# Experts of a top-1 mixture computed once each on 224 slots, with rows scattered to per-expert regions in DRAM

## The chip, the core and the metric

The kernel runs on one core of one Trainium2 chip. The metric is device time in microseconds (us) for one execution. Five engines work side by side, each with its own instruction queue: TensorE (PE; PEld is its weight load), VectorE (DVE), ScalarE (ACT), GpSimd (POOL) and SyncE (SP, which here only issues DMAs). Sixteen DMA engines move the data that the queues of SP, ACT and POOL ask for.

## The reference

Gated linear attention over 4 batches x 8 heads x 768 steps with head size 48, then a mixture of 16 experts in 4 groups of 4. Every one of 3072 tokens (rows of 384 numbers) goes to one expert, all in float32.

```python
for t in range(S):
    state = alpha[:, :, t, :, None] * state + np.einsum('bhd,bhe->bhde', k[:, :, t], v[:, :, t])
    y[:, :, t] = np.einsum('bhd,bhde->bhe', q[:, :, t], state)
x = y.transpose(0, 2, 1, 3).reshape(B * S, H * D)        # 3072 x 384

g_idx = np.argmax(x @ w_group, axis=1)                   # softmax weight g_w
e_idx = np.argmax(xg @ w_expert[g], axis=1)              # softmax weight e_w
h = np.maximum(xg[mask_e] @ w1[g, e], 0.0)               # 384 -> 1024
out[tok_idx] = (g_w * e_w)[:, None] * (h @ w2[g, e])     # 1024 -> 384
```

## The kernel before

**Attention.** Sixteen passes (a batch and a pair of heads each) run in a row. `load` brings q, k and alpha of a pass on SP's queue into one of two buffers. `decayed` forms the decay products: DVE scans alpha (line 150) and takes reciprocals, GpSimd makes `qp`, `ka` and half of `ks`, DVE makes `kp` and the rest. `scores`, `states` and `outputs` are matmuls on TensorE in chunks of 128 steps; `scores` needs `ka`, and `states` needs `ks`. Each matmul on float32 leaves two records in the trace. Results go to `x`, a tile of 128 rows x 6 chunks per batch, with two buffers.

**Gates.** After four passes `gates` computes a batch's routing: logits, the best group and expert, the weight (column 384 of `x`), `picked` (one-hot of 16) and `rank`, a token's place among those of its expert. The whole `x` of the batch is written to `x_dram` by one DMA from GpSimd (line 295).

**Slots.** When all tokens are ranked, DVE sorts them into 39 tiles of 128 slots: tile e below 16 has the first 128 tokens of expert e, and 23 more tiles take what is left of any expert, enough for every way in which the tokens can fall. Products of one-hots give the token of each slot (lines 400 to 425).

**Experts.** For every tile, GpSimd gathers its rows with an indirect DMA (`fetch_rows`, three tiles ahead), TensorE turns them (`turned`), and multiplies by `w1` (24 matmuls of 128 columns, line 466) and, after ReLU on ACT, by `w2` (8 matmuls of 384 columns, line 474). DVE scales the result into `yo`, and an indirect DMA scatters it to the output (line 479); slots without a token point beyond the output and write nothing. `load_weights` on SP's queue brings the weights of a tile, 1536 KB for each layer, into one of three buffers; the first three sets are requested during the attention passes. All 39 tiles are computed, whether they hold tokens or not.

**Order.** A scheduler in the library lays out each engine's queue ahead of time; it may move an instruction forward past others of its engine. Within a queue the order is then fixed. It also adds the waits: an instruction that writes what an earlier one wrote or reads waits for it, a DMA's write until it has landed.

Of the kernel before, what the change touches and what calls it, by code (L numbers as in the profile page):

```python
# [19 lines left out]
P = 128  # L20
# [4 lines left out]
def gla_then_hierarchical_moe(  # L25
# [9 lines left out]
    """Gated linear attention in chunks of 128 steps, then a top-1 of 4x4 expert MoE.  # L35

    The decay products restart every 64 steps, so that their reciprocals stay in range; a
    chunk's two segments are joined by the first one's whole decay.

    Tokens are sorted by expert into tiles of 128 slots: tile e < NE has the first 128 tokens of  # L40
    expert e, and the NX tiles after those have what is left of any expert, whose weights are
    fetched by its index. NX covers every way in which the tokens can fall.
    """
# [16 lines left out]
    NX = NT - 1  # L60
    NS = NE + NX
    XW = DM + 1
# [11 lines left out]

    x_dram = dp.tile([N, XW], F32, name="x_dram")
    x_rows = x_dram.rearrange("(b c p) w -> b p c w", b=B, p=P)

# [23 lines left out]
    lane_f = iota("lane_f", [P, P], [[1, P]])  # L101
    tile_f = iota("tile_f", [P, NT], [[1, NT]])
    full_f = iota("full_f", [P, NX], [[P, NX]], base=P)
# [6 lines left out]
    rank = cp.tile([P, NT], F32, name="rank")  # L110
    eid = cp.tile([P, NT], F32, name="eid")
# [15 lines left out]
    with ExitStack() as gla:  # L127
# [50 lines left out]
        def states(j, v, ks, tot):  # L178
            """The state before chunks 1, 2, ..., as blocks of the two heads."""
# [64 lines left out]
        def gates(b, x):  # L244
# [18 lines left out]
            def first_best(z, name):  # L263
                """The first best of four as one-hot, and the sum of exp(z - best)."""
# [30 lines left out]
            nc.gpsimd.dma_start(out=x_rows[b], in_=x)  # L295

            cs = slice(b * NC, (b + 1) * NC)
            ix = sp.tile([P, NC], F32, name="ix")
            nc.vector.tensor_scalar(out=ix, in0=gix[:, :, 0], scalar1=-4.0, scalar2=20.0,
                                    op0=ALU.mult, op1=ALU.add)  # L300
            nc.vector.tensor_tensor(out=eid[:, cs], in0=ix, in1=eix[:, :, 0], op=ALU.subtract)
# [19 lines left out]
            nc.vector.tensor_reduce(out=rank[:, cs], in_=rk, axis=AX.X, op=ALU.add)  # L321
# [10 lines left out]
        for j in range(PAIRS):  # L332
            b, hp = divmod(j, HP)
            if j + 1 < PAIRS:
                load(j + 1)
            if hp == 0:
                xs[b] = xp.tile([P, NC, XW], F32, name="x")
                if b + 1 < B:
                    load_v(b + 1)
            if j in (2, 4, 6):  # L340
                load_weights(j // 2 - 1, j // 2 - 1)
            qp, kp, qs, ks, ka, tot = decayed(j)
            sm = scores(0, qp, kp, ka)
            st = states(j, vs[b], ks, tot)
            for c0 in range(0, NC, 2):
                nxt = scores(c0 + 2, qp, kp, ka) if c0 + 2 < NC else None
                outputs(j, c0, sm, qs, st, vs[b], xs[b])
                sm = nxt
            if hp == HP - 1:
                gates(b, xs[b])  # L350

# [1 line left out]
    mp = ctx.enter_context(tc.tile_pool(name="moe", bufs=2))  # L353
    rp = ctx.enter_context(tc.tile_pool(name="route", bufs=1))

    cnt = seen[:, NT, :]
# [8 lines left out]
    base = rp.tile([P, NE], F32, name="base")  # L365
    nc.vector.tensor_tensor(out=base, in0=ends, in1=more, op=ALU.subtract)

# [5 lines left out]
    whose_i = rp.tile([P, NX], I32, name="whose_i")  # L373
    nc.vector.tensor_scalar(out=whose_i, in0=whose, scalar1=float(NE - 1), scalar2=None,
                            op0=ALU.min)

    turn3 = rp.tile([P, NT, NX], F32, name="turn3")
    nc.vector.tensor_tensor(out=turn3, in0=rank[:, :, None].to_broadcast([P, NT, NX]),
                            in1=full_f[:, None, :].to_broadcast([P, NT, NX]), op=ALU.is_ge)
    turn = rp.tile([P, NT], F32, name="turn")  # L380
    nc.vector.tensor_reduce(out=turn, in_=turn3, axis=AX.X, op=ALU.add)
    lo = rp.tile([P, NT], F32, name="lo")
    nc.vector.scalar_tensor_tensor(out=lo, in0=turn, scalar=-float(P), in1=rank, op0=ALU.mult,
                                   op1=ALU.add)
    own3 = rp.tile([P, NT, NE], F32, name="own3")
    nc.vector.tensor_tensor(out=own3, in0=picked, in1=base[:, None, :].to_broadcast([P, NT, NE]),
                            op=ALU.mult)
    hi = rp.tile([P, NT], F32, name="hi")
    nc.vector.tensor_reduce(out=hi, in_=own3, axis=AX.X, op=ALU.add)
    nc.vector.scalar_tensor_tensor(out=hi, in0=hi, scalar=float(NE - 1), in1=turn, op0=ALU.add,  # L390
                                   op1=ALU.add)
    late = rp.tile([P, NT], F32, name="late")
    nc.vector.tensor_scalar(out=late, in0=turn, scalar1=1.0, scalar2=None, op0=ALU.min)
    nc.vector.tensor_tensor(out=hi, in0=hi, in1=eid, op=ALU.subtract)
    nc.vector.tensor_tensor(out=hi, in0=hi, in1=late, op=ALU.mult)
    nc.vector.tensor_tensor(out=hi, in0=hi, in1=eid, op=ALU.add)

    # The token of each slot: a product of one-hots, whose numbers are whole and below 256.
    los = rp.tile([P, NT, P], BF16, name="los")
    nc.vector.tensor_tensor(out=los, in0=lo[:, :, None].to_broadcast([P, NT, P]),  # L400
                            in1=lane_f[:, None, :].to_broadcast([P, NT, P]), op=ALU.is_equal)
    his = rp.tile([P, NT, 3, NS], BF16, name="his")
    nc.vector.tensor_tensor(out=his[:, :, 0, :], in0=hi[:, :, None].to_broadcast([P, NT, NS]),
                            in1=lane_f[:, None, 0:NS].to_broadcast([P, NT, NS]), op=ALU.is_equal)
    nc.vector.tensor_scalar(out=his[:, :, 1, :], in0=his[:, :, 0, :], scalar1=part_f,
                            scalar2=None, op0=ALU.mult)
    nc.vector.tensor_tensor(out=his[:, :, 2, :], in0=his[:, :, 0, :],
                            in1=tile_f[:, :, None].to_broadcast([P, NT, NS]), op=ALU.mult)
    zs = bank()
    for t in range(NT):  # L410
        nc.tensor.matmul(zs[:, 0:3 * NS], lhsT=los[:, t, :],
                         rhs=his[:, t].rearrange("p k s -> p (k s)"), start=(t == 0),
                         stop=(t == NT - 1))
    slot = rp.tile([P, 3, NS], F32, name="slot")
    nc.vector.tensor_copy(out=slot, in_=zs[:, 0:3 * NS].rearrange("p (k s) -> p k s", k=3))
    tok = rp.tile([P, NS], F32, name="tok")
    nc.vector.scalar_tensor_tensor(out=tok, in0=slot[:, 2, :], scalar=float(P), in1=slot[:, 1, :],
                                   op0=ALU.mult, op1=ALU.add)
    src_i = rp.tile([P, NS], I32, name="src_i")
    nc.vector.tensor_copy(out=src_i, in_=tok)  # L420
    none = rp.tile([P, NS], F32, name="none")
    nc.vector.tensor_scalar(out=none, in0=slot[:, 0, :], scalar1=-float(N), scalar2=float(N),
                            op0=ALU.mult, op1=ALU.add)
    dst_i = rp.tile([P, NS], I32, name="dst_i")
    nc.vector.tensor_tensor(out=dst_i, in0=tok, in1=none, op=ALU.add)  # L425

# [1 line left out]
    def fetch_rows(i):  # L428
        xg = mp.tile([P, XW], F32, name="xg", bufs=4)
        nc.gpsimd.indirect_dma_start(  # L430
            out=xg, out_offset=None, in_=x_dram,
            in_offset=bass.IndirectOffsetOnAxis(ap=src_i[:, i:i + 1], axis=0),
            bounds_check=N - 1, oob_is_err=False)
        return xg

    def fetch_weights(i):
        if i < NE:
            return load_weights(i, i)
        e = nc.values_load(whose_i[0:1, i - NE:i - NE + 1], engines=[ENG.SP], min_val=0,
                           max_val=NE - 1,  # L440
                           skip_runtime_bounds_check_because="an index of one of NE")
        load_weights(i, e)

    def turned(xg):
        z = bank()
        for dc in range(DC):
            nc.tensor.transpose(z[:, dc * P:(dc + 1) * P], xg[:, dc * P:(dc + 1) * P], ident)  # L447
        xt = mp.tile([P, DC, P], F32, name="xgt")
        nc.vector.tensor_copy(out=xt.rearrange("p c t -> p (c t)"), in_=z[:, 0:DM])  # L449
        return xt  # L450

    AHEAD = 3
    rows = {i: fetch_rows(i) for i in range(AHEAD)}
    xt = turned(rows[0])
    for i in range(NS):
        if i + AHEAD < NS:
            rows[i + AHEAD] = fetch_rows(i + AHEAD)
        w1, w2 = weights.pop(i)
        xg = rows.pop(i)
# [62 lines left out]
```

## Time and profile before

| | |
|---|---|
| median of three runs | 971.7 us (971.56 to 972.98) |
| profiled execution: span from first to last instruction | 967.5 us |
| TensorE matmul busy | 862.4 us, 89% |
| VectorE busy | 314.5 us, 33% |
| GpSimd busy | 148.9 us, 15% |
| bytes moved by DMA | 159.4 MB |

The profile is of one execution, and its page gives the span alone as that execution's own time; the runs are timed around the whole program. Busy times are per engine and overlap. A stretch of the span is read from a table of windows, a single place from the timeline, and the time that a DMA takes from its issue to its landing from the list of DMAs.

### The profile page before, as it was taken

How to read it: one execution, taken by the hardware profiler on the slowest of the kernel's cores; microseconds unless marked ns; L12 is line 12 of the kernel's file. 1: busy time of each engine (PE TensorE's matmuls, PEld its weight loads, DVE VectorE, ACT ScalarE, POOL GpSimd, SP SyncE). 2: the span in 40 equal slices, each digit the busy share in tenths (PEclk: the TensorE clock that was granted, in tenths of full speed). 3: DMA queues.
4: the chain of work that ended last, by engine and by line, in shares of the span. 5: the costliest groups of instructions: out<-in, count | busy, mean ns of one | idle time of the engine just before them, and what ended most of it. 6: DMA issues, size and time to landing. Idle time of an engine off the chain costs nothing. (4 is left out here: it accounts for less than half of the span.)

```text
span 967.5 us, 10908 instructions
## 1 busy us (share of the span) xinstructions
PE 862.4 (89%) x4413; PEld 695.5 (72%) x4413; DVE 314.5 (33%) x785; ACT 91.8 (9%) x211; POOL 148.9 (15%) x151
## 2 busy tenths in 40 slices
PE   0499987999879998699991999999999999999996
PEld 0377775777757777477781788877887788778884
DVE  0856656345563454934316010101011010101010
ACT  0000010000100001000010001100111001100110
POOL 2211111101111010110001122111211121111200
PEclk9999999999999999555555999999999999999998
DMA  9732233202331022300001689988998888999940
GB/s 331 202 103 37 37 85 87 38 0 38 86 85 38 1 37 37 87 1 0 1 1 63 212 317 332 329 324 326 325 334 316 325 307 326 314 314 316 317 164 1
DMA packets 20130, 159.44 MB, mean 165 GB/s; under 512 B 3976, under 2 KB 4022, under 8 KB 8048
## 3 DMA queue, kind: packets, MB, share of 16 engines
q1 hardware_dynamic: 13280, 136.85, 43.8%
q0 software_dynamic: 6080, 17.15, 5.0%
q10 hardware_dynamic: 720, 4.75, 1.3%
q8 instruction: 35, 0.57, 0.2%
q14 instruction: 15, 0.12, 0.1%
HBM read 149.28 MB, written 12.40 MB: 167 GB/s over the span
## 5 line engine op out<-in xcount | busy, mean ns | idle before, releaser
L466 PEld LDWEIGHTS bank<-xgt,w 128*128 128x128 f32 x1872 | 216.8, 193 | 11.1 <-DVE xgt L449 1.1
L466 PE MATMUL bank<-xgt,w 128*128 128x128 f32 x1872 | 217.2, 276 | 0.7 <-DVE xgt L449 0.7
L474 PE MATMUL bank<-w,hT 128*128 128x384 f32 x624 | 207.7, 486 | 0.0
L214 PE MATMUL bank<-qp,kp 48*128 48x128 f32 x384 | 147.1, 498 | 35.1 <-DVE tot L175 35.1
L474 PEld LDWEIGHTS bank<-w,hT 128*128 128x128 f32 x624 | 115.5, 190 | 72.3
L214 PEld LDWEIGHTS bank<-qp,kp 48*128 48x128 f32 x384 | 92.5, 308 | 59.7 <-issue 38.6
L237 PE MATMUL bank<-v,sm 128*128 128x48 f32 x384 | 98.0, 401 | 0.0
L237 PEld LDWEIGHTS bank<-v,sm 128*128 128x128 f32 x384 | 93.0, 329 | 4.8 <-issue 1.6
L479 POOL DMA_INDIRECT out_dram<-yo,dst_i x39 | 39.6, 1016 | 340.7 <-DVE yo L477 340.7
L216 PE MATMUL bank<-qp,ka 48*64 48x64 f32 x384 | 87.5, 337 | 0.1
L449 DVE COPY xgt<-bank 128x384 f32<-128x384 f32 x39 | 21.7, 558 | 200.3 <-PE bank L447 200.3
L220 DVE TENSOR_TENSOR sm<-bank,causal 128x256 f32<-128x256 f32 x96 | 39.8, 421 | 142.4 <-PE bank L216 141.1
L468 ACT ACTIVATE hT<-bank 128x512 f32<-128x512 f32 x78 | 46.6, 597 | 397.3 <-PE bank L466 397.3
L477 DVE TENSOR_SCALAR yo<-bank,xg 128x384 f32<-128x384 f32 x39 | 24.1, 618 | 184.9 <-PE bank L474 184.9
L216 PEld LDWEIGHTS bank<-qp,ka 48*64 48x64 f32 x384 | 52.6, 200 | 39.8 <-issue 38.1
L152 DVE RECIPROCAL inv<-cum 112x768 f32<-112x768 f32 x16 | 79.2, 4952 | 0.5
L155 POOL TENSOR_TENSOR qp<-qka,cum 112x768 f32<-112x768 f32 x16 | 28.9, 1805 | 216.1 <-issue 81.3
L232 PE MATMUL bank<-state,qs 112*128 112x96 f32 x160 | 53.9, 456 | 0.0
L150 DVE TENSOR_TENSOR_SCAN cum<-qka,zeros 112x64 f32<-112x64 f32 x192 | 41.8, 272 | 25.4 <-DMA qka<-in_qka_dram 25.4
L194 PE MATMUL bank<-v,kn 128*112 128x96 f32 x160 | 39.9, 415 | 9.0 <-ACT kn L190 9.0
L194 PEld LDWEIGHTS bank<-v,kn 128*112 128x112 f32 x160 | 32.3, 298 | 16.4 <-ACT kn L190 14.6
L430 POOL DMA_INDIRECT xg<-x_dram,src_i x39 | 39.6, 1014 | 28.0 <-DVE dst_i L425 16.4
(108 smaller groups left out, 432.5 us busy)
## 6 DMA issues: line engine op xcount, KB each, us to landing
w<-in_w_dram SPq DMA_DIRECT2D x78, 1536.0 KB, 9.1
qka<-in_qka_dram SPq DMA_DIRECT2D x32, 432.0 KB, 7.0
x_dram<-x POOLq DMA_DIRECT2D x4, 1155.0 KB, 6.4
v<-in_v_dram ACTq DMA_DIRECT2D x4, 1152.0 KB, 9.1
xg<-x_dram,src_i POOLq DMA_INDIRECT x39, 7.3
out_dram<-yo,dst_i POOLq DMA_INDIRECT x39, 7.9
wr<-in_wr_dram ACTq DMA_DIRECT2D x1, 30.0 KB, 7.1
```

Source lines behind the costliest of these rows:

```text
L150: nc.vector.tensor_tensor_scan(out=cum[:, sl], data0=a[:, sl], data1=zeros[0:R], initial=1.0, op0=ALU.mult, op1=ALU.add)
L152: nc.vector.reciprocal(out=inv, in_=cum)
L194: nc.tensor.matmul(z[0:R, c * D2:(c + 1) * D2], lhsT=kn[:, i, :], rhs=v[:, c, hp * D2:(hp + 1) * D2], start=True, stop=True)
L214: nc.tensor.matmul(z[:, o:o + P], lhsT=kp[r, c:c + P], rhs=qp[r, c:c + P], start=True, stop=True)
L216: nc.tensor.matmul(z[0:SEG, o + SEG:o + P], lhsT=ka[r, c // 2:c // 2 + SEG], rhs=qp[r, c + SEG:c + P], start=True, stop=True)
L220: nc.vector.tensor_tensor(out=s, in0=z[:, 0:2 * P].rearrange("p (c i) -> p c i", c=2), in1=causal[:, None, :].to_broadcast([P, 2, P]), op= ...
L232: nc.tensor.matmul(z[:, i * D2:(i + 1) * D2], lhsT=qs[:, c * P:(c + 1) * P], rhs=st[0:R, c - 1, :], start=True, stop=False, skip_group_che ...
L237: nc.tensor.matmul(z[:, i * D2 + t * D:i * D2 + (t + 1) * D], lhsT=sm[t][:, i, :], rhs=v[:, c, h * D:(h + 1) * D], start=(c == 0 and t == ...
L430: nc.gpsimd.indirect_dma_start(out=xg, out_offset=None, in_=x_dram, in_offset=bass.IndirectOffsetOnAxis(ap=src_i[:, i:i + 1], axis=0), bou ...
L466: nc.tensor.matmul(z[:, k * P:(k + 1) * P], lhsT=w1[:, dc, f * P:(f + 1) * P], rhs=xt[:, dc, :], start=(dc == 0), stop=(dc == DC - 1))
L468: nc.scalar.activation(out=hT[:, f0:f0 + 4, :].rearrange("p f t -> p (f t)"), in_=z, func=AF.Relu)
L474: nc.tensor.matmul(zy[:, 0:DM], lhsT=hT[:, f, :], rhs=w2[:, f, :], start=(f == 0), stop=(f == FC - 1))
```

## The change

- `x` gets a second extra column with the token's number. The write of `x` to `x_dram` goes. `gates` now computes `place` = expert x 3072 + rank for each token, and six indirect DMAs per batch scatter the rows of `x` to `slots_d`, a region of 3072 rows per expert in DRAM.
- The first 224 rows of each of these regions are set to zero beforehand by one DMA from `blank`, written in the pass j = 1.
- The one-hot routing goes. Each expert is computed once, on the first 224 rows of its region, in parts of 128 and 96 rows, which plain DMAs on ACT's queue load. `hidden` runs w1 on 224 columns at once, with four evictions of 448 columns; `result` runs w2 for each part. `drop` sends slots beyond an expert's count past the end of the output.
- Tokens of an expert beyond 224 are left to a loop with a run-time count, a tile of 128 rows per pass. Its bookkeeping stands on DVE.

```diff
-    NX = NT - 1
-    NS = NE + NX
-    XW = DM + 1
+    CAP = 224
+    NX = -(-(N - CAP) // P)
+    XW = DM + 2
-    x_dram = dp.tile([N, XW], F32, name="x_dram")
+    slots_d = dp.tile([NE * N, XW], F32, name="slots_d")
+    blank = cp.tile([P, 2 * XW], F32, name="blank")
+    nc.vector.memset(blank, 0.0)
...
-            nc.gpsimd.dma_start(out=x_rows[b], in_=x)
+            nc.vector.tensor_copy(out=x[:, :, DM + 1], in_=token_f[:, cs])
...
+            nc.vector.scalar_tensor_tensor(out=place, in0=ix, scalar=float(N), in1=rank,
+                                           op0=ALU.mult, op1=ALU.add)
+            for c in range(NC):
+                nc.gpsimd.indirect_dma_start(
+                    out=slots_d, out_offset=bass.IndirectOffsetOnAxis(ap=place[:, c:c + 1], axis=0),
+                    in_=x[:, c, :], in_offset=None, bounds_check=NE * N - 1, oob_is_err=False)
...
+            if j == 1:
+                nc.sync.dma_start(
+                    out=slots_d.rearrange("(e n) w -> e n w", e=NE)[:, 0:CAP, :].rearrange(
+                        "e (p t) w -> p e (t w)", t=2),
+                    in_=blank[0:CAP // 2, None, :].to_broadcast([CAP // 2, NE, 2 * XW]))
...
+    def hidden(w1, xt, n):
+        hT = mp.tile([P, FC, CAP], F32, name="hT")
+        for f0 in range(0, FC, 2):
+            z = bank()
+            for k in range(2):
+                f = f0 + k
+                for dc in range(DC):
+                    nc.tensor.matmul(z[:, k * n:(k + 1) * n], lhsT=w1[:, dc, f * P:(f + 1) * P],
+                                     rhs=xt[:, dc, 0:n], start=(dc == 0), stop=(dc == DC - 1))
+            nc.scalar.activation(out=hT[:, f0:f0 + 2, 0:n],
+                                 in_=z[:, 0:2 * n].rearrange("p (f t) -> p f t", f=2), func=AF.Relu)
...
+    halves = [(0, P), (P, CAP - P)]
+    def fetch_rows(e):
+        xg = mp.tile([P, 2, XW], F32, name="xg", bufs=4)
+        for t, (c0, n) in enumerate(halves):
+            nc.scalar.dma_start(out=xg[0:n, t, :], in_=slots_d[e * N + c0:e * N + c0 + n, :])
...
+    for e in range(NE):
+        if e + AHEAD < NE:
+            rows[e + AHEAD] = fetch_rows(e + AHEAD)
...
+        hT = hidden(w1, xt, CAP)
+        if e + 1 < NE:
+            xt = columns(rows[e + 1])
+        for t, (c0, n) in enumerate(halves):
+            result(w2, hT, c0, n, xg[0:n, t, DM:DM + 1], dst[0:n, t:t + 1])
+        if e + 3 < NE:
+            load_weights(e + 3, e + 3)
...
+    n_left = nc.values_load(n_more[0:1, 0:1], min_val=0, max_val=NX,
+                            skip_runtime_bounds_check_because="a count of at most NX")
+    with tc.For_i(0, n_left) as i:
...
```

The queue of SP at the program's start, before. `w` is a weight tile of either layer, `qka` the tile of q, k and alpha:

```order
L120 DMA w_383<-in_w_dram 128x3072
L122 DMA w_384<-in_w_dram 128x3072
L120 DMA w_753<-in_w_dram 128x3072
L141 DMA qka_114<-in_qka_dram 48x2304 [waits Pool_49]
L141 DMA qka_114<-in_qka_dram 48x2304
```

The same place in SP's queue after the change:

```order
L120 DMA w_386<-in_w_dram 128x3072
L348 DMA slots_d<-blank 112x16x772 [waits DVE_49]
L141 DMA qka_116<-in_qka_dram 48x2304 [waits Pool_49]
L141 DMA qka_116<-in_qka_dram 48x2304
```

The zeroing of the slots stands second, although it is written in pass j = 1, and two of the weight transfers stand behind the first `qka` loads.

GpSimd's queue in the passes behind the third batch, before; `Pool`, `DVE`, `PE` and `Activation` in the waits are engines, DMASW and DMAHW semaphores of DMAs:

```order
L169 TENSOR_TENSOR ka<-kp,cum 112x384 [waits DVE_49]
L295 DMA x_dram<-x 128x6x385 [waits DVE_49,Activation_49]
L171 TENSOR_TENSOR ks<-ka,cum 112x6x64 [waits Pool_49]
L155 TENSOR_TENSOR qp<-qka_114,cum 112x768 [waits DMAHW0_49,DMAHW7_49,DVE_49,PE_49]
L169 TENSOR_TENSOR ka<-kp,cum 112x384 [waits DVE_49]
L171 TENSOR_TENSOR ks<-ka,cum 112x6x64 [waits Pool_49]
```

The same passes after the change, up to the six scatters of the last batch (the first two of them are shown):

```order
L171 TENSOR_TENSOR ks<-ka,cum 112x6x64 [waits Pool_49]
L326 DMA slots_d<-x,place 49152x386 [waits DMASW3_49,DVE_49,Activation_49]
L326 DMA slots_d<-x,place 49152x386 [waits DMASW4_49]
L155 TENSOR_TENSOR qp<-qka_116,cum 112x768 [waits DMAHW0_49,DMAHW1_49,DVE_49,PE_49]
L326 DMA slots_d<-x,place 49152x386 [waits DMASW5_49,Activation_49]
L326 DMA slots_d<-x,place 49152x386 [waits DMASW6_49]
L326 DMA slots_d<-x,place 49152x386 [waits DMASW7_49,Activation_49]
L169 TENSOR_TENSOR ka<-kp,cum 112x384 [waits DVE_49]
L171 TENSOR_TENSOR ks<-ka,cum 112x6x64 [waits Pool_49]
L326 DMA slots_d<-x,place 49152x386 [waits DMASW0_49]
```

One DMA has become six, with `qp`, `ka` and `ks` of the next pass between them, and each scatter waits for the semaphore of the DMA before it. The last batch's six stand in a row behind the last `ks`. TensorE's order in the attention passes is the same in both kernels.

## Rows read from the trace of the kernel before

**Rows 1.** Windows: us; busy us (x records) of PE, PEld, DVE, ACT, POOL; clock, DMA share, GB/s
```profile
0.00:25.00 25.00, 0.00 (x0) 0.00 (x0) 0.07 (x1) 1.28 (x1) 7.09 (x21) 1.00 0.93 326
...
100.00:200.00 100.00, 89.72 (x366) 72.93 (x366) 51.51 (x147) 9.05 (x27) 13.62 (x12) 1.00 0.27 60
420.00:440.00 20.00, 19.51 (x79) 15.36 (x78) 5.97 (x21) 2.32 (x7) 0.84 (x1) 0.50 0.00 1
600.00:700.00 100.00, 100.00 (x625) 80.79 (x624) 11.20 (x19) 10.75 (x18) 19.29 (x19) 1.00 0.90 322
```

**Rows 2.** Timeline, program start: start, length (us), engine, line, operation, count [idle before]
```profile
0.83 0.40 SPq L120 DMA_DIRECT2D w<-in_w_dram  x1
...
1.76 0.42 SPq L120 DMA_DIRECT2D w<-in_w_dram  x1
...
4.95 3.80 SPq L141 DMA_DIRECT2D qka<-in_qka_dram  x4
...
26.38 2.29 DVE L150 TENSOR_TENSOR_SCAN cum<-qka,zeros 112x64 f32<-112x64 f32 x12 [25.41 <-DMA qka<-in_qka_dram]
```

**Rows 3.** DMAs of three windows (200:300, 400:520, 520:545): count, KB, median us to landing
```profile
v<-in_v_dram ACTq DMA_DIRECT2D x1, 1152.0 KB, 5.0
...
x_dram<-x POOLq DMA_DIRECT2D x1, 1155.0 KB, 5.8
...
xg<-x_dram,src_i POOLq DMA_INDIRECT x4, 3.1
```

**Rows 4.** All out scatters (line 479), then all gathers (line 430)
```profile
DMA to landing us min/median/max: 2.1/7.9/10.5
...
DMA to landing us min/median/max: 3.1/7.3/11.4
```

**Rows 5.** Timeline around the third batch's gates, DVE, POOL and PE
```profile
399.44 0.24 DVE L321 TENSOR_REDUCE rank<-rk 128x6 f32<-128x96 f32 x1
...
413.17 1.81 POOL L155 TENSOR_TENSOR qp<-qka,cum 112x768 f32<-112x768 f32 x1 [16.14 <-PE bank L216]
419.12 0.84 POOL L169 TENSOR_TENSOR ka<-kp,cum 112x384 f32<-112x384 f32 x1 [4.14 <-DVE kp L156]
...
424.24 0.47 PE L216 MATMUL bank<-qp,ka 48*64 48x64 f32 x2
```

**Rows 6.** Timeline from the last gates to the first expert tile
```profile
513.52 0.24 DVE L321 TENSOR_REDUCE rank<-rk 128x6 f32<-128x96 f32 x1
...
528.36 1.09 POOL L430 DMA_INDIRECT xg<-x_dram,src_i  x1 [16.39 <-DVE dst_i L425]
529.76 1.03 POOL L430 DMA_INDIRECT xg<-x_dram,src_i  x1 [0.31 <-issue]
...
533.24 7.37 PE L466 MATMUL bank<-xgt,w 128*128 128x128 f32 x48 [0.65 <-DVE xgt L449]
```

**Rows 7.** Timeline of PE: two places in the attention stage, then one expert tile
```profile
155.23 0.79 PE L214 MATMUL bank<-qp,kp 48*128 48x128 f32 x2
...
430.94 0.79 PE L214 MATMUL bank<-qp,kp 48*128 48x128 f32 x2
...
545.93 5.52 PE L466 MATMUL bank<-xgt,w 128*128 128x128 f32 x48
551.29 0.49 PE L447 MATMUL bank<-ident,xg 128*128 128x128 f32 x3
551.62 5.33 PE L474 MATMUL bank<-w,hT 128*128 128x384 f32 x16
556.78 0.49 PE L466 MATMUL bank<-xgt,w 128*128 128x128 f32 x3
```

**Rows 8.** Timeline of the end
```profile
956.52 1.45 PE L474 MATMUL bank<-w,hT 128*128 128x384 f32 x4
...
958.90 0.98 POOL L479 DMA_INDIRECT out_dram<-yo,dst_i  x1 [9.53 <-DVE yo L477]
```

**Rows 9.** Drains of POOL at the program's end: ns min/median/max, first to last start (us)
```profile
L518 POOLq DRAIN  x3: 40/107/7993, 958.7 to 967.2; - x3
```

## The prediction before the change was run

> **What bounds the kernel now.** I read the busy shares by stretch first [rows 1]. Three limits follow one another. In the first 25 us TensorE does nothing, while the DMA engines are 93% busy at 326 GB/s. From 100 to 200 us the attention stage keeps TensorE busy for 89.7 of 100 us. From 600 to 700 us, in the expert stage, it is busy for 100.0 of 100 us, with 322 GB/s beside it. A transfer is therefore the limit at the start, and TensorE in both stages. Between the stages it waits for routing [rows 6]. The clock column reads 1.00 (2.4 GHz) at 100 to 200 us and 0.50 (1.2 GHz) at 420 to 440 us, yet two matmul records of the score line L214 take 0.79 us at both places [rows 7]. For the attention stage I therefore let the clock column decide nothing.
>
> **The sum, part by part.** The profiled span is 967.5 us. The median of the three runs is 971.7 us, 4.2 us more; I make the sum on the span and add 4.2 us at the end.
>
> *Experts: -102.3 us.* Before, a tile costs one period on TensorE [rows 7]: 24 first-layer matmuls on 128 columns take 551.29 - 545.93 = 5.36 us (223 ns each), 3 transposes 0.33 us, and 8 second-layer matmuls on 384 columns take 556.78 - 551.62 = 5.16 us (645 ns each). Over 39 tiles that is 39 x 5.36 + 38 x 0.33 + 39 x 5.16 = 422.8 us, plus 1.8 us because the first tile's 48 records, coming after a wait, take 7.37 instead of 5.52 us [rows 6, 7]. Started at 533.24, that ends at 957.8, and the last matmuls do end at 957.97 [rows 8]. After, an expert costs 24 matmuls on 224 columns, 6 transposes and 16 matmuls on 384 columns. No row has 224 columns; between 223 ns at 128 and 645 ns at 384 the line gives 381 ns, so 24 x 381 = 9.15 us. The halves cost 2 x 5.16 = 10.32 us: 96 tokens in the second half narrow the stationary side and leave 384 streamed columns. Six transposes are about 0.58 us. That is 16 x 9.15 + 15 x 0.58 + 16 x 10.32 = 320.2, with the same slow beginning 322.0 us, against 424.6: -102.6. I take -102.3, as the 96-row transposes may cost a little more than their share. If the 224-column matmul scaled with columns alone it would be 390 ns and cost 3.5 us more. What hides the rest: each expert has 3 MB of weights to fetch per 20 us, and now 122 MB of weights become 50 MB; before, 3 MB came every 10.85 us and TensorE still did not wait. Four ReLU evictions per expert are spread over 9.15 us. On ACT the two row loads stand ahead of the next ReLUs and can wait for the last yo; the first ReLU is due only 2.3 us after that.
>
> The counts come from the inputs, not from the profile: computed with the reference, the experts hold 158 to 213 tokens. All fit in 224, so the counted loop should run zero times. The profile agrees as far as it can: some out scatters land in 2.1 us, where the median is 7.9 [rows 4], as the empty tiles among the 39 would.
>
> *Start: +7.3 us.* Three weight transfers of 1536 KB stand on SP's queue ahead of the first q, k, alpha load at 4.95 us, and the first scan starts at 26.38 us after 25.41 us of waiting for that load [rows 2]. The change puts the zeroing of the slots second in that queue: 112 x 16 rows of 3088 bytes, 5.53 MB, while two weight transfers, 3.15 MB, move behind the load. So 2.39 MB more stand ahead of it; at 326 GB/s [rows 1] that is 7.3 us, and nothing covers it. No row shows a write of this shape. Above: the only large write, 1155 KB in 5.8 us [rows 3], gives 204 GB/s with its latency, so the zeroing would take 27.1 instead of 17.0 us and the term be +17.5. Below: a gain is excluded, as bytes are only added. I take the queue's own rate because a transfer this long hides its latency.
>
> *Scatters in the attention stage: +0.7 us.* One 1155 KB write per batch becomes six indirect DMAs on GpSimd. Each waits until the one before has landed, since all write slots_d, and between them stand ka and ks, which TensorE needs. The price is the landing time L from issue. The first gathers of 128 rows, unloaded, land in 3.1 us [rows 3]; the shortest scatter, taken as an empty one, in 2.1, and scatters beside weight traffic in 7.9 at the median and 10.5 at most [rows 4]. Here the DMA engines are idle (1 GB/s at 420 to 440 us [rows 1]), so I take 3.1, and 0.35 us to the next issue (0.30 between consecutive DMAs [rows 6]). For batches 0 and 1 only the second scatter stands ahead of ka, with over 2 us to spare. For batch 2, place is ready at about 400, two scatters go before qp at 413.17, and three stand between qp's end at 415.0 and ka (419.12 before) [rows 5]. With L = 3.1 they end at 423.1 and ka at 424.0; TensorE wants it at 424.24 [rows 5], and ks a little later, about 0.7 us late. Each further microsecond of L costs 2 us here: 9 to 10 us at L = 7.9.
>
> *Between the stages: +7.0 us.* Before, rank starts at 513.52, a long one-hot routing follows, the first gather starts at 528.36, and first-layer matmuls start at 533.24 [rows 6]. After, place is ready about 0.5 us behind rank's end, at 514.3, and the first scatter goes at 514.7. Six in a row: 514.7 + 5 x 3.45 + 3.1 = 535.05. Only then may ACT load the rows. No row shows an unloaded load of 198 KB; 1152 KB took 5.0 us and the shortest scatter 2.1 [rows 3, 4], and I take 2.7, landing at 537.9. The old way from landing (531.46) to first matmul was 1.8 us, and the second half adds 0.5: 540.2, which is 7.0 late. Each microsecond of L costs 6 us here. All routing arithmetic that leaves DVE was part of the old 15 us; the loop's bookkeeping lies on DVE beside the scatters.
>
> The Trainium skill, "DMA: Bandwidth & Descriptors", section on the anatomy of a SWDGE DMA, puts such a DMA at about 2.0 us plus bytes over 436 GB/s; my estimate from it for 198 KB is 2.45 us, which would make the total 5 us shorter. The trace has 3.1 us for a gather of that size [rows 3], and that decides.
>
> *End: +3.1 us.* Before, the last scatter starts at 958.90, and GpSimd's drain, 7.99 us long, governs the end [rows 8, 9]. After, the last scatter carries rows: +1.1 (3.1 against 2.1, rounded). Each engine then reads a count and branches over the loop, with one or two more barriers. No row shows that; the barrier behind the drain took 0.8 us (966.7 to the span's end), so I take two and a little, +2.0. Bounds: 0, if it runs beside the drain; +8, if a second drain of that length follows.
>
> Sum: 7.3 + 0.7 + 7.0 - 102.3 + 3.1 = -84.2. The span becomes 883.3 and the time **887.5 us**.
>
> **Rivals.** *A, long landings.* If scatters into slots_d land as out scatters do (L = 7.9), 4.8 us x (6 + 2) = +38 us: about 926. Against it: DMA traffic is absent where they run. For it: these rows lie in sixteen regions, and no scatter with data has an unloaded row. *B, slow zeroing.* The write goes at 204 GB/s or less: +10 us, 898. *C, slower than before.* The same chain, but so long that it eats the gain. Place: GpSimd's queue; price: 8 us per microsecond of L, and about 10 once batches 0 and 1 delay ka too; 84.2 / 10 = 8.4, so it decides from L of about 11.5, giving 972 and, at 13, about 986. The longest landing of any indirect DMA in this trace is 11.4 us, beside full weight traffic [rows 4]. *D, not what it says.* An expert with over 224 tokens makes the loop run, with weights, rows, and about 11 us of matmuls in series, some 25 us per pass: 912 with one pass. The inputs speak against it. *E, another pace in the attention stage.* The same matmuls run faster in the expert stage than there; were the attention stage to leave the pace that it keeps at both readings of the clock, it could gain tens of microseconds, down to DVE's 51.5 of 100 us [rows 1]. Nothing in the change touches its order of matmuls, so I give no time beyond 'below 877'.
>
> **How the numbers follow.** Forecast 78%, A (with milder forms, L from 5) 8%, B 8%, C 2%, D 1%, E 2%, a time within 0.2% of before 1%. The likely case with its bounds reaches from 877 (an end hidden, L of 2.5) to about 900; B lies inside up to 899, and mild forms of A lead to 906. I give 877 to 906. About 0.2% is what a measurement of this kernel can tell from no change. Faster: 0.97; same: 0.01; slower: 0.02.
>
> **What would show it.** First scan at 33 to 34 us. Six scatters spaced 3.4 to 3.6 us after the fourth batch's place. First L390 matmul 14 to 16 us later than the old first L466. An expert period of 20.0 us, TensorE busy throughout. A prediction of this kind fails if the spacing is twice that, if the zeroing runs under 250 GB/s, or if TensorE waits inside the expert stage.

## The result, and the profile after

The changed kernel takes 883.7 us (median of 4, 883.18 to 884.08) against 972.0 us: a ratio of 0.909, 95% interval 0.9077 to 0.9103. I predicted 887.5 us, in a range of 877 to 906. Its profiled execution has a span of 882.3 us.

In some executions TensorE runs one batch's gates 1 to 3 us faster than in the rest, and the profiled execution of before was such a one (below, before_again); a second profile of it has a span of 970.1 us, and I count against that.

The windows of the changed kernel, with the columns of [rows 1]:

```profile
0.00:25.00 25.00, 0.00 (x0) 0.00 (x0) 0.91 (x3) 1.28 (x1) 7.09 (x22) 1.00 0.92 348
25.00:35.00 10.00, 0.00 (x0) 0.00 (x0) 0.00 (x0) 0.00 (x0) 0.00 (x0) 1.00 1.04 251
100.00:200.00 100.00, 89.71 (x366) 72.69 (x364) 57.28 (x154) 9.74 (x29) 17.98 (x16) 1.00 0.29 67
...
600.00:700.00 100.00, 100.00 (x431) 76.42 (x431) 12.12 (x32) 10.84 (x21) 9.51 (x10) 1.00 0.52 191
```

TensorE is still the limit in both stages, and beside it the experts' DMA traffic fell from 322 to 191 GB/s. At the start TensorE and VectorE stand empty almost nine microseconds longer. The timeline of the changed kernel, at the places of [rows 2, 5 to 8] (start, length, engine, line, operation, count, idle before):

```profile
1.79 0.34 SPq L348 DMA_DIRECT2D slots_d<-blank  x1
4.95 19.33 SPq L141 DMA_DIRECT2D qka<-in_qka_dram  x4
...
35.07 2.29 DVE L150 TENSOR_TENSOR_SCAN cum<-qka,zeros 112x64 f32<-112x64 f32 x12 [32.27 <-DMA qka<-in_qka_dram]
...
434.11 0.97 POOL L326 DMA_INDIRECT slots_d<-x,place  x1 [2.48 <-ACT x L241]
435.09 0.85 POOL L169 TENSOR_TENSOR ka<-kp,cum 112x384 f32<-112x384 f32 x1
436.00 0.47 PE L216 MATMUL bank<-qp,ka 48*64 48x64 f32 x2
...
522.50 0.26 PE L310 MATMUL bank<-picked,before 128*128 128x96 bf16 x1 [4.01 <-DVE picked L307]
526.66 1.01 POOL L326 DMA_INDIRECT slots_d<-x,place  x1 [45.70 <-DVE n_more L478]
529.67 0.97 POOL L326 DMA_INDIRECT slots_d<-x,place  x1 [2.00 <-DMA slots_d<-x,place]
...
542.53 0.97 POOL L326 DMA_INDIRECT slots_d<-x,place  x1 [2.14 <-DMA slots_d<-x,place]
545.23 3.70 ACTq L413 DMA_DIRECT2D xg<-slots_d  x8
...
550.10 11.77 PE L390 MATMUL bank<-xt_e,w 128*128 128x224 f32 x48 [0.55 <-DVE xt_e L379]
562.28 10.51 PE L399 MATMUL bank<-w,hT 128*128 128x384 f32 x32
572.62 9.24 PE L390 MATMUL bank<-xt_e,w 128*128 128x224 f32 x48
...
592.63 7.54 PE L390 MATMUL bank<-xt_e,w 128*128 128x224 f32 x39
...
867.60 4.68 PE L399 MATMUL bank<-w,hT 128*96 128x384 f32 x14
```

The same marks in the second profile of before:

```profile
513.79 0.26 PE L311 MATMUL bank<-picked,before 128*128 128x96 bf16 x1 [4.01 <-DVE picked L308]
536.31 3.96 PE L466 MATMUL bank<-xgt,w 128*128 128x128 f32 x21 [0.65 <-DVE xgt L449]
...
955.32 5.33 PE L474 MATMUL bank<-w,hT 128*128 128x384 f32 x16
```

The two timelines give the prediction's sum term by term. The bridge reaches from the last `picked` to the first w1 matmul (550.10 - 522.50 = 27.60 us now, 536.31 - 513.79 = 22.52 before), and the end from TensorE's last matmul to the end of the span (882.3 - 872.28 and 970.1 - 960.65):

| term | predicted | measured | from |
|---|---|---|---|
| start, first scan | +7.3 | +8.7 | 35.07 - 26.38 [rows 2], the same in the second profile |
| attention, to the last `picked` | +0.7 | 0.0 | 522.50 - 513.79 = 8.71, the start alone |
| bridge, `picked` to first w1 matmul | +7.0 | +5.1 | 27.60 - 22.52 |
| experts, to TensorE's end | -102.3 | -102.2 | (872.28 - 550.10) - (960.65 - 536.31) |
| end, to the span's end | +3.1 | +0.6 | 10.02 - 9.45 |
| sum | -84.2 | -87.8 | 882.3 - 970.1 |

### The profile page after: what moved, and what is told of

It reads as the page before. It is cut to its first block, busy times and chain, and to the rows that moved or that the text cites. A ratio compares the mean times of both kernels' runs of the same rounds, so it can differ in the third digit from the quotient of the medians.

```text
span 882.3 us, 8155 instructions
## 1 busy us (share of the span) xinstructions
PE 760.9 (86%) x3152; PEld 601.2 (68%) x3152; DVE 301.5 (34%) x805; ACT 80.0 (9%) x197; POOL 121.5 (14%) x126
## 5 line engine op out<-in xcount | busy, mean ns | idle before, releaser
L214 PE MATMUL bank<-qp,kp 48*128 48x128 f32 x384 | 147.1, 498 | 43.8 <-DVE tot L175 43.8
L399 PE MATMUL bank<-w,hT 128*96 128x384 f32 (+1 forms) x512 | 168.2, 487 | 0.0
L390 PEld LDWEIGHTS bank<-xt_e,w 128*128 128x128 f32 x768 | 147.2, 193 | 5.7 <-issue 2.4
L390 PE MATMUL bank<-xt_e,w 128*128 128x224 f32 x768 | 150.4, 356 | 0.5 <-DVE xt_e L379 0.5
L214 PEld LDWEIGHTS bank<-qp,kp 48*128 48x128 f32 x384 | 92.5, 308 | 68.3 <-issue 47.3
L399 PEld LDWEIGHTS bank<-w,hT 128*96 128x96 f32 (+1 forms) x512 | 89.2, 177 | 70.0 <-issue 38.3
L402 DVE TENSOR_SCALAR yo<-bank,xg 128x384 f32<-128x384 f32 (+1 forms) x32 | 19.7, 615 | 154.1 <-PE bank L399 154.1
L404 POOL DMA_INDIRECT out_dram<-yo,dst x32 | 30.4, 950 | 300.2 <-DVE yo L402 300.2
L392 ACT ACTIVATE hT<-bank 128x448 f32<-128x448 f32 x64 | 34.8, 543 | 306.4 <-PE bank L390 306.4
L232 PEld LDWEIGHTS bank<-state,qs 112*128 112x128 f32 x160 | 41.3, 327 | 3.0 <-issue 1.1
L241 ACT COPY x<-bank 128x192 f32<-128x192 f32 x48 | 15.3, 320 | 275.6 <-PE bank L237 275.6
## 6 DMA issues: line engine op xcount, KB each, us to landing
slots_d<-blank SPq DMA_DIRECT2D x1, 5404.0 KB, 27.3
```

The source lines that it names most:

```text
L214: nc.tensor.matmul(z[:, o:o + P], lhsT=kp[r, c:c + P], rhs=qp[r, c:c + P], start=True, stop=True)
L232: nc.tensor.matmul(z[:, i * D2:(i + 1) * D2], lhsT=qs[:, c * P:(c + 1) * P], rhs=st[0:R, c - 1, :], start=True, stop=False, skip_group_che ...
L390: nc.tensor.matmul(z[:, k * n:(k + 1) * n], lhsT=w1[:, dc, f * P:(f + 1) * P], rhs=xt[:, dc, 0:n], start=(dc == 0), stop=(dc == DC - 1))
L392: nc.scalar.activation(out=hT[:, f0:f0 + 2, 0:n], in_=z[:, 0:2 * n].rearrange("p (f t) -> p f t", f=2), func=AF.Relu)
L399: nc.tensor.matmul(zy[0:n, 0:DM], lhsT=hT[:, f, c0:c0 + n], rhs=w2[:, f, :], start=(f == 0), stop=(f == FC - 1))
L404: nc.gpsimd.indirect_dma_start(out=out, out_offset=bass.IndirectOffsetOnAxis(ap=dst, axis=0), in_=yo[0:n], in_offset=None, bounds_check=N ...
```

## Experiments

All times are medians; differences are against the changed kernel's 883.7 us unless said otherwise.

### Where the expert stage's gain comes from

**before_32.** The kernel before, with the seven empty tiles left out:

```diff
-    NX = NT - 1
+    NX = NE
```

> The kernel before with 32 tiles instead of 39: the seven tiles left out hold no token with these counts. Theory (the gain of the change is TensorE columns, 39 tiles of 10.85 us against 16 experts of 20 us): 7 x 10.85 = 76 us less than before, about 896, so that three quarters of the 102.6 us gained in the expert stage are the empty tiles, and the rest, 26.6 us, are the 32 padding columns that each expert has fewer in the first layer. Rival (the gain comes from fetching each expert's weights once, not twice): the seven tiles are cheap, since they only stand in the shadow of 3 MB of weights each, and the time stays above 920.

893.1 us, a ratio to before of 0.918 (0.9163 to 0.9202), so 79 us less than before. Its timeline, first and last matmuls of the stage:

```profile
534.14 7.17 PE L466 MATMUL bank<-xgt,w 128*128 128x128 f32 x48 [0.65 <-DVE xgt L449]
...
877.42 5.33 PE L474 MATMUL bank<-w,hT 128*128 128x384 f32 x16
```

The stage takes 882.75 - 534.14 = 348.6 us, 75.7 less than before. The other 3 us lie mostly in the bridge, whose one-hots are smaller (`picked` to first matmul 20.78 instead of 22.52), and in a shorter end (8.35 instead of 9.45). The rival, that the extra tiles stood in the shadow of weights, falls. Three quarters of the stage's gain are tiles that held no token; merging the rest gains 26.4 us (348.6 to 322.2), and the start, the bridge and the end give 17 of these back, so that the whole change beats this one-line edit by 9.4 us. The edit holds for these counts alone, though, while the changed kernel keeps the loop for any others.

**cap256.** More slots for every expert:

```diff
-    CAP = 224
+    CAP = 256
```

> CAP is 256 instead of 224; nothing else is changed. Theory (TensorE's time for the first layer goes by streamed columns, on the line of the prediction, 1.65 ns per column): 24 matmuls x 32 columns x 1.65 ns x 16 experts = 20.2 us, about 1 us for wider transposes, and 2 to 4 us at the start for 0.77 MB more of zeroing: 907 to 909. If columns alone counted, without the line's fixed part (390 ns at 224, 446 at 256): 21.5 us for the first term. Rival (an expert's cost is set by weights and whole tiles, so that 224 and 256 columns cost the same): 886 to 888.

904.5 us, 20.8 more. A period's w1 matmuls, grouped on the timelines of cap256, and of cap192 (below):

```profile
570.88 10.52 PE L390 MATMUL bank<-xt_e,w 128*128 128x256 f32 x48
```

```profile
832.84 8.07 PE L393 MATMUL bank<-xt_e,w 128*128 128x192 f32 x48
```

With 5.52 us at 128 columns [rows 7] and 9.24 at 224, that is 5.52, 8.07, 9.24, 10.52 us for 128, 192, 224, 256 columns: each column costs 1.5 to 1.7 ns a matmul, the prediction's line. The rival, whole tiles, falls. The 0.79 MB more of zeroing cost nothing at the start: the first scan is at 34.83 us, against 35.07 in the changed kernel, and there my expectation was 2 to 4 us too high. More bytes ahead did delay the load, though: in the traces its first packet moves at 28.2 us instead of 26.3, and the load itself then took less time. Why it did stays open.

### What the start costs

**late_zero.** The zeroing moves behind the second pass's `decayed`, and its source waits for that pass:

```diff
-            if j == 1:
-                nc.sync.dma_start(out=slots_d..., in_=blank...)
...
+            if j == 1:
+                nc.vector.tensor_scalar(out=blank[0:R, 0:1], in0=tot[:, 0, :], scalar1=0.0, ...)
+                nc.sync.dma_start(out=slots_d..., in_=blank...)
```

> The zeroing is kept whole, but its source depends on a value of the second pass, so that the first q, k and alpha loads stand ahead of it on SP's queue. Theory (the 8.7 us by which the first scan is later are the wait of those loads behind the zeroing): the first scan goes back from 35.07 to about 26.4 us, the zeroing lands inside the attention stage, and the time falls by 8 to 9 us, to about 875. Rival 1 (the bytes cost the same wherever they go, because loads of a later pass now wait behind the zeroing and TensorE for them): the first scan goes back, a wait of 5 to 9 us appears ahead of the fourth pass's scan, and the time stays within 3 us of 884. Rival 2 (the start is late for another cause, as the order of the first two weight transfers): the first scan stays at 35 us.

880.7 us, 3.1 less. The first scan did go back, to 25.49 us, but two thirds of that were lost again. Timeline:

```profile
58.13 0.33 SPq L353 DMA_DIRECT2D slots_d<-blank  x1
...
103.83 2.29 DVE L150 TENSOR_TENSOR_SCAN cum<-qka,zeros 112x64 f32<-112x64 f32 x12
...
112.52 0.76 PE L214 MATMUL bank<-qp,kp 48*128 48x128 f32 x2 [3.79 <-DVE tot L175]
```

TensorE waits for the fourth pass, whose load stands behind the zeroing on SP's queue. **later_zero** places it behind `states` of the second pass and lets it wait for a state instead, so that this load goes first:

```diff
-                nc.vector.tensor_scalar(out=blank[0:R, 0:1], in0=tot[:, 0, :], scalar1=0.0, ...)
+                nc.vector.tensor_scalar(out=blank[0:R, 0:1], in0=st[0:R, NC - 2, 0:1], scalar1=0.0, ...)
```

> As late_zero, but the zeroing's source now depends on a state of the second pass, so that it stands on SP's queue behind the load of the fourth pass and not ahead of it. Theory (what late_zero lost again, 6.5 us of the 9.6 that its first scan gained, is that one load: behind the zeroing SP's four issues took from 58.6 to 80.4 us, and TensorE then waited 3.8 us for the fourth pass): the first scan stays at 25 to 26 us, no wait on tot behind the first, and the time is 8 to 9.5 us under the changed kernel, about 875. Rival (the 5.5 MB cost their DMA time whatever stands behind them): 3 us again, about 881.

874.7 us, 9.0 less: all of the start's 8.7. First scan and the fourth pass's scans:

```profile
25.98 2.29 DVE L150 TENSOR_TENSOR_SCAN cum<-qka,zeros 112x64 f32<-112x64 f32 x12 [23.20 <-DMA qka<-in_qka_dram]
...
82.24 0.28 DVE L150 TENSOR_TENSOR_SCAN cum<-qka,zeros 112x64 f32<-112x64 f32 x1
...
89.01 1.92 DVE L150 TENSOR_TENSOR_SCAN cum<-qka,zeros 112x64 f32<-112x64 f32 x10
```

So the 5.5 MB cost nothing that shows where nobody waits behind them. No run puts the zeroing on another queue at the start, so what the shared DMA engines add is not measured by itself; but ACT's loads of v, on their own queue beside the zeroing, landed no later than before. Changed kernel, then before (KB each, median us to landing):

```profile
v<-in_v_dram ACTq DMA_DIRECT2D x2, 1152.0 KB, 10.3
```

```profile
v<-in_v_dram ACTq DMA_DIRECT2D x2, 1152.0 KB, 13.1
```

My reading of late_zero in that expectation was half wrong: the 21.8 us were a group of four issues with a buffer wait in it. The load had landed by about 81 us (two halves, 16.9 and 21.5 us after their issues at 64.5 and 58.6). What made DVE late is its order: the scans that later_zero has in DVE's pauses from 82 us on stand in late_zero in one piece at 103.83, behind the evictions. The scheduler laid the queue out that way; that it did so because it reckoned with a late load is an inference.

### What the bridge costs

**one_wait.** The last batch's scatters (their rows are disjoint) go out without waiting for each other:

```diff
...
+            else:
+                with tc.tile_critical():
+                    placed = nc.alloc_semaphore("placed")
+                    for c in range(NC):
+                        scatter(c).then_inc(placed, 16)
+                    nc.gpsimd.wait_ge(placed, 16 * NC)
```

> The last batch's six scatters are issued one behind the other and waited for once; the rows they write are disjoint. Theory (between the stages the time goes to waiting for each landing before the next issue, 6 x 3.17 us from 526.7 to 545.2): six issues of about 1.0 us each and one landing of 2.6 us, so the rows load about 9 to 10 us earlier and the time falls by 8 to 10 us, to about 875. Rival (the issues are not what waits: the writes of 128 rows themselves take the 3 us each on the DMA side, one behind the other): the spacing stays near 3 us and the time falls by under 2 us. GpSimd's extra wait for other engines at the section's head may take back up to 1 us.

876.3 us (872.5 to 877.2), 7.5 less; in the profiled execution the span is 8.2 us shorter, of which the bridge gives 6.6 and the end 1.7. Timeline:

```profile
523.19 0.26 PE L310 MATMUL bank<-picked,before 128*128 128x96 bf16 x1 [4.00 <-DVE picked L307]
527.68 1.01 POOL L326 DMA_INDIRECT slots_d<-x,place  x1 [46.03 <-issue]
...
534.11 0.97 POOL L326 DMA_INDIRECT slots_d<-x,place  x1 [0.31 <-issue]
539.30 3.70 ACTq L423 DMA_DIRECT2D xg<-slots_d  x8
...
544.19 11.21 PE L400 MATMUL bank<-xt_e,w 128*128 128x224 f32 x48 [0.55 <-DVE xt_e L389]
```

The spacing falls from 3.17 to (534.11 - 527.68) / 5 = 1.29 us: what stood between the issues was the wait for the landing. The rival falls. The bridge gains less than the 9 to 10 us expected, because an issue takes 1.29 and not 1.0 us, the section starts 0.3 us later, and the loads follow 5.19 us behind the last issue instead of 2.70. Most of that last part is a side effect of the critical section (`tile_critical`): at its end GpSimd runs a drain of 2.04 us (from 537.10), and the loads go at 539.30. In exchange the drain at the program's end is 2.66 us instead of 4.65, which is why the end is shorter too.

**twice.** Every scatter is issued two times:

```diff
-            for c in range(NC):
+            for c in [c for c in range(NC) for _ in range(2)]:
                 nc.gpsimd.indirect_dma_start(
```

> Each of the 24 scatters into the slots is issued twice, with the same rows, so that every chain of them is twice as long. Theory (only the last batch's chain lies on the path, 3.17 us a scatter; those of the attention passes lie beside TensorE's work, though in the third batch ka is ready only 0.06 us before TensorE wants it): 6 x 3.17 = 19.0 us for the last batch, and for the attention passes between nothing and 9.5 us (three more scatters ahead of one ka): 903 to 912. Rival (a landing costs so much because each scatter is the first after a pause, and a second one straight behind it is quicker): under 12 us in all, 895 or less. Rival (scatters in the attention passes delay ka in every batch, as the prediction's case C has it, 8 to 10 us for each microsecond of landing): above 915.

903.6 us (901.2 to 906.5), 19.9 more, at the theory's lower end; both rivals fall. The last batch's twelve scatters, first and last:

```profile
527.09 1.01 POOL L326 DMA_INDIRECT slots_d<-x,place  x1 [45.69 <-DVE n_more L478]
...
561.28 0.97 POOL L326 DMA_INDIRECT slots_d<-x,place  x1 [2.11 <-DMA slots_d<-x,place]
```

That is 34.19 / 11 = 3.11 us a scatter, 18.7 us for six more. The span of this profile is 22.4 us longer: besides the 18.7 the end grows by 2.7, of which GpSimd's drain is 2.0 (below). The last `picked` stands 0.4 us later (522.93), as does the first scan, so twelve scatters per batch still cost the attention passes nothing. This is weaker than it looks: the scheduler spread the doubled scatters anew, and in the third batch `ka` again has three ahead of it.

### What the loop costs

**no_loop.** The loop and its bookkeeping are left out:

```diff
-    over = rp.tile([P, NE, NX], F32, name="over")
...
-    with tc.For_i(0, n_left) as i:
...
```

> The counted loop at the end and its bookkeeping are left out; with these counts it has nothing to do. The prediction's reading (an empty loop costs TensorE's end about 2 us in barriers, and nothing elsewhere): 2 us less, all behind the last matmul. The trace of the changed kernel (tail 10.0 us against 9.5 before): at most 0.5 to 1 us less behind the last matmul; and about 1 us less ahead of the first scatter, where over, more and ends (0.54, 0.53 and 0.18 us) stand between DVE's ranks and places. Together 1 to 2 us, about 882.

878.8 us (875.98 to 881.29), 4.9 less; its profiled execution is 3.2 us shorter in span (879.1), and I go by that, as its four times spread over 5.3 us. Its last matmul ends at 871.77, so the end takes 7.33 us instead of 10.02: the empty loop costs 2.7 us there, near the 2.0 of the prediction and not the 0.5 to 1 that I had then read from the trace. The first scatter follows `picked` by 3.30 instead of 4.16 us, 0.9 us as expected.

**cap192.** Nine experts have tokens left (RS takes the place of N wherever a region's length counts; all 320 rows of a region are zeroed, at later_zero's place):

```diff
-    CAP = 224
+    CAP = 192
+    RS = CAP + P
...
-    slots_d = dp.tile([NE * N, XW], F32, name="slots_d")
+    slots_d = dp.tile([NE * RS, XW], F32, name="slots_d")
```

> CAP is 192, so that nine experts have tokens left (200 to 213 of them) and the counted loop runs nine times; the regions are cut to 320 rows, all of them zeroed, at the place of later_zero. Columns saved: 24 x 32 x 1.65 ns x 16 = 20.2 us; start: 8 us saved. Theory of the prediction's rival D (a pass is serial: index, 3 MB of weights, 24 matmuls on 128 columns, 8 on 384, eviction, scatter, barrier; some 25 us): 884 - 28 + 9 x 25 = 1081, and 1054 to 1117 for passes of 22 to 29 us. Rival (a pass overlaps with the one before, and costs the 10.9 us of its matmuls): about 955.

1122.8 us, so above the range, and for two reasons that the total mixes. The passes themselves lie inside it: from the last expert's matmul at 870.69 us to the last pass's at 1115.71 nine passes take 245.0 us, 27.2 each. One pass on the timeline:

```profile
910.48 0.87 PE L380 MATMUL bank<-ident,xg 128*128 128x128 f32 x3 [16.05 <-DMA xg<-slots_d,src]
...
925.73 1.01 POOL L407 DMA_INDIRECT out_dram<-yo,to  x1 [21.28 <-DVE yo L405]
929.47 0.38 DVE L498 MEMSET xg<- 128x386 f32 x1 [4.02 <-PEq L485]
...
937.60 0.87 PE L380 MATMUL bank<-ident,xg 128*128 128x128 f32 x3 [12.81 <-DMA xg<-slots_d,src]
```

Serial indeed: 15.2 us of computation, 3.7 from the scatter to the next pass, 8.1 for rows beside 3 MB of weights. (The first pass takes 30.1 us; GpSimd's drain behind it lasts 5.8 us, behind the later ones 2.3.) A pass costs more than the 20.0 us of a whole expert in the changed kernel. An expert's period with 192 columns is 19.31 us (852.15 - 832.84), so 32 slots fewer save 11 us on all sixteen, not the 20 expected, and pay for less than half a pass.

The rest is a loss of 18.7 us in the attention stage: the last `picked` stands at 532.57 us, and at 513.9 in later_zero. Here the scheduler put four of the first batch's scatters ahead of the next pass's `qp` on GpSimd's queue and the other two ahead of its `ka`, and TensorE waited:

```profile
166.31 0.76 PE L215 MATMUL bank<-qp,kp 48*128 48x128 f32 x2 [17.33 <-DVE tot L176]
176.24 0.47 PE L217 MATMUL bank<-qp,ka 48*64 48x64 f32 x2 [9.17 <-POOL ka L170]
```

That is the mechanism of the prediction's case C, once, with landings of 2.6 us at the least and 8.5 at most: what it costs depends on how many scatters the scheduler lays ahead of what TensorE needs, and not on the landing alone.

### Is before always as its profile showed?

**before_again.** The kernel before, unchanged.

> The kernel before, unchanged, profiled once more. Its profile that the prediction read has a span of 967.5 us, and spans stand 1.7 us under times elsewhere, so that execution was about 969.2, 2.4 us under the fastest time shown. Theory: that execution alone ran the third batch's gates faster (36 router matmuls in 5.26 us, where the other batches take 8), and a second profile shows 8 us there and a span of 970 to 971.5. Rival: the kernel before does this in every execution, and the changed kernel has lost 3 us there: 5.3 us again and a span near 967.5.

971.9 us, with a span of 970.1. The router matmuls (L258) of the third batch, in the first profile and then in the second (columns: PE, PEld, clock, DMA share, GB/s):

```profile
340.00:420.00 80.00, 5.26 (x36) 5.21 (x36) 0.77 0.24 48
```

```profile
340.00:420.00 80.00, 7.93 (x36) 8.00 (x36) 1.00 0.23 48
```

The rival falls: the changed kernel lost nothing in the gates. Against the first profile its last `picked` seems 11.75 us late; all of the shift is there already at 406 us, right behind the third batch's gates.

The clock records of the traces say more. In the first profile they begin at 379.9 us with 1.00 (2.4 GHz) and fall to 0.50 (1.2 GHz) at 383.3, and the faster matmuls lie there. The same twelve records, first profile and second:

```profile
379.95 1.41 PE L258 MATMUL bank<-wr,xt 128*128 128x20 f32 x12
```

```profile
379.94 2.59 PE L258 MATMUL bank<-wr,xt 128*128 128x20 f32 x12
```

Ahead of a trace's first clock record the column reads 1.00 with no record behind it. In the changed kernel the first record starts at 555.0 us, inside the expert stage's first group of w1 matmuls: that group takes 11.77 us, the later ones 9.24, and the 2.5 us lost are half of the 4.9 us that lie ahead of the record. So the 1.00 that the prediction read at 100 to 200 us [rows 1] is no measured clock, and its comparison of L214 at two readings [rows 7] does not show that the clock makes no difference there. That the attention stage runs at 1.2 GHz but for these few microseconds fits all of this; no record shows it, and why the clock rises in some executions only stays open.

### All of it

**together.** The edits of later_zero and of one_wait, and

```diff
-    CAP = 224
+    CAP = 216
```

> The zeroing as in later_zero, the last batch's scatters under one wait as in one_wait, and CAP 216, which still holds every expert's tokens with these counts. Theory (the three costs lie one behind the other on the path and don't touch each other): 9.0 us from later_zero, 6.6 to 7.5 us from one_wait, and 24 x 8 columns x 1.65 ns x 16 experts = 5.1 us, together 20.7 to 21.6 us under the changed kernel: 862 to 863. Rival (part of the bridge's wait is hidden behind something that only comes to light when the chain is shorter, as the first weights or TensorE's slow first matmuls): 865 to 870.

861.1 us (858.33 to 861.88), 22.6 less than the changed kernel and 0.885 of before (0.8825 to 0.888), 1 us under the range expected. The three costs add up, and the rival falls. With 216 columns every expert still fits (213 at most).

## Why the prediction was right, and what was off

**What bounds, and the experts:** right. TensorE is busy for 100.0 of 100 us, an expert takes 592.63 - 572.62 = 20.0 us, and a 224-column matmul 9.24 / 24 = 385 ns, where the line gave 381. The 96-token half streams about as long as the full one, as the prediction took it: the two together take 10.51 us, and one full one took 5.33 [rows 7]. The slow beginning was 2.5 us and not 1.8, since more of it lay ahead of the clock's rise.

**Start:** right in place, 1.4 us short. In the traces the load's first packet moves at 26.3 us and moved at 19.4 before, so the bytes ahead cost 6.9 us, near the 7.3 of the sum; the load itself then took 8.8 us instead of 7.0, for a reason that stays open. The zeroing was 27.3 us on its way, 203 GB/s, so the prediction's sign of failure, under 250, came true. It did no harm, because the load behind the zeroing did not wait for its landing (at 29.1 us). later_zero shows that the whole term is this write ahead of the load.

**Scatters in the attention stage:** 0.7 predicted, 0.0 measured, by a hair. `ka` ends at 435.94 and TensorE takes it at 436.00 without a gap; `ks`, which the sum had late, was not: TensorE takes it at 436.40. (GpSimd's record of `ks` ends at 436.86, so these ends are good to half a microsecond at best.) The mechanism stood, but that the term is nothing is luck of the order that the scheduler laid out: in cap192 another order cost 18.7 us.

**Bridge:** 7.0 predicted, 5.1 measured. Two terms were too large: the spacing, 3.17 instead of 3.45 us, five times, and the way from the last scatter to the first matmul, 7.57 us instead of 8.25, where 0.15 is a slip in the sum (535.05 + 2.7 is 537.75, not 537.9). The first scatter stood where I had it, 1.2 us behind `rank`. The nearest row, the 3.1 us gather, misled me a little: the list of DMAs gives 2.6 to 2.8 us for the six scatters of the bridge. The Trainium skill, "DMA: Bandwidth & Descriptors", on the anatomy of a SWDGE DMA, from which I had estimated 2.45 us, was nearer here; the trace stands 0.15 to 0.35 us above that estimate.

**End:** 3.1 predicted, 0.6 measured, the largest miss in share. The loop's part was about right (2.0 against 2.7, no_loop). Wrong was the other part, +1.1 for a last scatter that carries rows: without the loop the end is 2.1 us *shorter* than before (7.33 against 9.45). What I had not asked is what GpSimd's drain waits for. It is shorter with fewer DMAs of GpSimd (below), and the change has 56 of them instead of 82; without the loop it is 5.82 us instead of 7.99, which is the 2.1.

**Span and time.** The five terms together are 3.6 us short (-84.2 against -87.8). That the span came out only 1.0 us from the 883.3 predicted is luck: the profile that the sum starts from was 2.6 us shorter than the second one, by its faster gates. Of the 4.2 us added at the end 1.7 separate any execution's time from its span, and the rest was this.

**Rivals.** A and C needed landings of 5 us and more where TensorE waits; the bridge's scatters landed in 2.6 to 2.8 us, and the longest of the 24, 7.5 us, fell in the first batch and held nothing up. B's rate occurred (203 GB/s) without its price. D did not occur; a pass would have cost 27 and not 25 us. E: the pace did change, in five of the twelve profiles, but for one batch's gates only, and its condition, equal pace at both readings of the clock, rested on a column without records.

## What to carry to other kernels

Count what the limiting engine does for nothing before counting what can be merged: here tiles without a token were three quarters of the gain in that stage, and one line would have taken most of it. A large write that nobody reads for 100 us still holds up a small load that stands behind it on the same queue; put it behind the load, and look at where the scheduler then places its users, as the same DMAs cost nothing in one order and 18.7 us in another. And when writes to one buffer are disjoint, one wait for all of them in place of a wait for each gave 7 us at a single place. Before a column of the profile carries an argument, check that records stand behind it.

## What the runs showed of the hardware

In these runs the length of GpSimd's drain goes by how many DMAs it had issued since its drain before. The longest of three drains at the program's end, in before_32, no_loop, the changed kernel, twice and one_wait, in this order (ns min/median/max):

```profile
L518 POOLq DRAIN  x3: 40/107/6848, 883.4 to 890.8; - x3
```

```profile
L475 POOLq DRAIN  x3: 40/102/5817, 872.5 to 878.8; - x3
```

```profile
L540 POOLq DRAIN  x3: 40/103/4649, 876.8 to 882.0; - x3
```

```profile
L540 POOLq DRAIN  x3: 44/103/6609, 897.3 to 904.4; - x3
```

```profile
L550 POOLq DRAIN  x3: 51/252/2661, 870.2 to 873.8; - x3
```

Without a loop, 82, 68 and 56 indirect and plain DMAs of GpSimd give 7.99 [rows 9], 6.85 and 5.82 us; with the loop, 80 and 56 give 6.61 and 4.65. That is 82 to 86 ns for each DMA in all three steps. one_wait, with 56 too, has a drain of 2.04 us behind its 24 scatters into the slots and one of 2.66 behind its 32 output scatters, 83 to 85 ns each again: the time was split, and not saved.

SP needed 19.33 us for four issues behind the zeroing's 1792 rows, against 3.80 before [rows 2], and 16.17 behind the 2048 rows of cap256: an issue is not free behind a long write, but the number of rows alone does not set its price. And the output scatters landed in 2.6 us at the median instead of 7.9 [rows 4], with weight traffic at 191 instead of 322 GB/s beside them.
